# The last output tile of a two-layer MLP kernel in two column pieces, 320 and 128 wide

## Chip, cores and metric

The kernel runs on one core of one Trainium2 chip. It is written instruction by instruction: each engine has its own list of work, and semaphores order the lists against one another. The metric is the device time of one execution in microseconds (us). Four executions of the kernel before gave 93.84, 93.88, 93.94 and 94.49 us; the median is 93.91 us.

The engines are TensorE (PE in the profile; its weight loads are PEld), VectorE (DVE), ScalarE (ACT), GpSimd (POOL) and SyncE (SP, which issues most transfers here).

## What is computed

```python
B, S, D, F = 1, 2048, 448, 1792      # all tensors bf16
def reference(x, w1, b1, w2, b2):
    h = jnp.einsum("bsd,df->bsf", x, w1) + b1
    h = jax.nn.gelu(h, approximate=True)
    return jnp.einsum("bsf,fd->bsd", h, w2) + b2
```

## The kernel before

The 2048 rows of x are worked in four chunks of 512 (`SC`). Layer 1 of a chunk forms h transposed, with 14 blocks of 128 hidden features on the partitions and 512 rows along the free dimension. ScalarE takes each block out of PSUM with the Gelu and the bias b1 into `g`. Layer 2 multiplies: an output tile has 128 rows of x on its partitions and 448 columns; for each of the 14 feature blocks, 128 columns of `g` are the stationary weights and a row block of `w2_sb` streams through.

**Row halves.** TensorE is used as two halves of 64 rows each, which work side by side. Every product over 128 features is made of two matmuls over 64 features. In a part "a" of Layer 2, bank 0 of the tile's PSUM unit gets its products from row half 0 and bank 1 from row half 1; in part "b" it is the other way round. The two matmuls of a step are issued one behind the other and run at the same time, each with a weight load of its own. `mm` (L209) adds a wait where a bank goes from one half to the other. PSUM has four such units of two banks, given out in turn by `next_unit`.

**Layer 2 of the last chunk** sets the end. Its four tiles are p (tiles 0 and 1, a bank for each), q (tile 2) and r (tile 3). In q and r the 448 columns of one tile are split over the two banks, 224 in each. TensorE's order is written out at L438 to L445: p.a, q.a, p.b, then r's bias product, r.a, q.b, r.b. So the drains and stores of p and q run while TensorE is still busy.

**The drain of r.** When r.b ends, VectorE adds b2 to the first 224 columns (L326) while ScalarE copies the other 224 (L329). ScalarE cannot add a row vector in that copy, so b2 is added into this bank ahead of time by a matmul: `bias` (L286) multiplies a matrix of ones with `b2_z`, a tile that is zero but for one row, which is b2. It uses row half 1, and that row is row 64, filled by VectorE at L424 as soon as b2 has been loaded. When both drains are done, SP issues one store for the tile (L275, called at L331) of 128 rows of 896 B, and the program ends when all stores have arrived (L446).

VectorE, ScalarE and SP each work in the order of their lists. SP's list at the end is the two stores of p, the store of q, the store of r.

Of the kernel before, what the change touches and what calls it, by code (L numbers as in the profile page):

```python
# [6 lines left out]
ALU = mybir.AluOpType  # L7
# [66 lines left out]
def bass_standalone__dense_activation_gelu__prompt_kernel(  # L74
# [8 lines left out]
    B, S, D = x.shape  # L83
    F = w1.shape[1]
    P = 128
    H = P // 2
# [3 lines left out]
    x2, out2 = x[0], out[0]  # L90
    NSC, NST, STC, NFT = S // SC, S // P, SC // P, F // P
# [2 lines left out]
    D3 = KT * P  # L94
    DH = D // 2
    NWARM = 7

    with ExitStack() as es:
        sb = lambda name, shape, dt: es.enter_context(nc.sbuf_tensor(name, shape, dt))
# [6 lines left out]
        w2_sb = sb("w2_sb", [P, NFT, D], BF16)  # L106
# [4 lines left out]
        b2_bc = sb("b2_bc", [P, D], BF16)  # L111
        b2_z = sb("b2_z", [P, D], BF16)
        g = sb("g", [P, NFT, S], BF16)
        out_sb = sb("out_sb", [P, NST, D], BF16)
        unit = [es.enter_context(nc.psum_tensor(f"u{i}", [P, 2, SC], FP32)) for i in range(4)]

        pr = Program(nc, es)
        one = nc.const_aps.tensor(1.0, [P, 1], BF16)
        ones_w = one.broadcast_to([P, P])
# [32 lines left out]
        o0v = out2[0:SC, :].rearrange("(p t) d -> p t d", t=STC)  # L152
# [9 lines left out]
        for c in range(1, NSC):  # L162
            for slot in range(KT + 1):
# [5 lines left out]
            out=ident[:, :], in_=ident[:, :], compare_op=ALU.not_equal, fill=1.0,  # L169
# [4 lines left out]
               after=["b1z"])  # L174
# [11 lines left out]
        def dup_x(s0, s1, after, event):  # L186
            pr.op("vector", lambda e: e.tensor_copy(xT[0:H, KT, s0:s1], xT[H:P, KT, s0:s1]),  # L187
                  after=after, event=event)

        def warm(n, cols=SC):  # L190
            for _ in range(n):
                pr.op("tensor", lambda e: e.matmul(unit[0][:, 0, 0:cols], lhsT=ones_w, rhs=ones_m[:, 0:cols],  # L192
                                                   start=True, stop=True))
# [7 lines left out]
        def next_unit():  # L201
            u = order[0]
            order[0] = (u + 1) % 4
            return u

        def free(u):
            return [busy[(u, i)] for i in (0, 1, 2) if (u, i) in busy]

        def mm(u, lo, half, cols, lhsT, rhs, start, stop, after, event=None, skip=False):  # L209

            after = list(after)
            before = side.get((u, lo))
            if start:
                before = None
            if before is not None and before[0] != half:
                after.append(before[1])
            o = pr.op("tensor", lambda e: e.matmul(  # L217
                unit[u][:, lo, cols], lhsT=lhsT, rhs=rhs, start=start, stop=stop, skip_group_check=skip),
                after=after, event=event)
            side[(u, lo)] = (half, o)  # L220

        class Layer1:


            def __init__(self, c, j):
                self.c, self.j, self.u, self.fresh = c, j, next_unit(), True
                self.skip = c == 0
# [43 lines left out]
                        bias=b1_f[:, ft:ft + 1], scale=1.0), after=[("h", c, ft), "b1"], event=("g", c, ft))  # L271
                    busy[(u, lo)] = ("g", c, ft)

        def store(j, after):
            pr.dma("sync", lambda e: e.dma_start(o0v[:, j, :] if j < STC else out2[j * P:(j + 1) * P, :], out_sb[:, j, :]), "out", after=after)  # L275

        class Layer2:


            def __init__(self, c, tiles, last=False):  # L280
                self.c, self.tiles, self.last, self.u = c, tiles, last, next_unit()
                self.split = len(tiles) == 1
                self.n = DH if self.split else D
                self.fresh = [True, True]

            def bias(self):  # L286
                mm(self.u, 1, 1, slice(0, DH), ones_w[H:P, :], b2_z[H:P, DH:D], True, False, free(self.u) + ["b2z"])
                self.fresh[1] = False

            def part(self, name, fts):  # L290
                c, u, n = self.c, self.u, self.n
                for ft in fts:
                    for lo in (0, 1):
                        j = c * STC + self.tiles[0 if self.split else lo]
                        half = lo if name == "a" else 1 - lo
                        rows = slice(half * H, (half + 1) * H)
                        d0 = lo * DH if self.split else 0
                        fin = name == "b" and ft == NFT - 1
                        after = [("g", c, ft), ("w2", ft - ft % 7)] + (free(u) if self.fresh[lo] else [])
                        mm(u, lo, half, slice(0, n), g[rows, ft, j * P:(j + 1) * P], w2_sb[rows, ft, d0:d0 + n],  # L300
                           self.fresh[lo], fin, after, ("y", c, self.tiles[0], lo) if fin else None)
                        self.fresh[lo] = False
                if name == "b" and NFT - 1 in fts:
                    self.drain()

            def drain(self):
                c, u = self.c, self.u
                y = [("y", c, self.tiles[0], lo) for lo in (0, 1)]
                if not self.split:
                    for lo in (0, 1):  # L310
                        j = c * STC + self.tiles[lo]
                        pr.op("vector", lambda e, lo=lo, j=j: e.tensor_tensor(  # L312
                            out=out_sb[:, j, :], in0=unit[u][:, lo, 0:D], in1=b2_bc[:, :], op=ALU.add),
                            after=[y[lo], "b2"], event=("o", j))
                        busy[(u, lo)] = ("o", j)
                        store(j, [("o", j)])
                    return
                j = c * STC + self.tiles[0]
                if not self.last:
                    pr.op("vector", lambda e: e.tensor_tensor(  # L320
                        out=out_sb[:, j, :].rearrange("p (two h) -> p two h", two=2), in0=unit[u][:, :, 0:DH],
                        in1=b2_bc[:, :].rearrange("p (two h) -> p two h", two=2), op=ALU.add),
                        after=y, event=("o", j))
                    store(j, [("o", j)])
                else:
                    pr.op("vector", lambda e: e.tensor_tensor(  # L326
                        out=out_sb[:, j, 0:DH], in0=unit[u][:, 0, 0:DH], in1=b2_bc[:, 0:DH], op=ALU.add),
                        after=[y[0]], event=("o", j, 0))
                    pr.op("scalar", lambda e: e.copy(out_sb[:, j, DH:D], unit[u][:, 1, 0:DH]),  # L329
                          after=[y[1]], event=("o", j, 1))  # L330
                    store(j, [("o", j, 0), ("o", j, 1)])  # L331

# [53 lines left out]

        warm(NWARM)
        warm(1, HC)  # L390
# [5 lines left out]
        for i in (0, 1):  # L396
# [3 lines left out]
                  after=[("w1r", i)], event=("w1rU", i))  # L400
# [13 lines left out]
        for c in range(NSC):  # L414
            if c:
                items = [Layer1(c, j) for j in range(NPAIR)]
                items[0].a()
                for j in range(1, NPAIR):
                    items[j].a()
                    items[j - 1].b()  # L420
                items[-1].b()
            else:

                pr.op("vector", lambda e: e.tensor_copy(b2_z[H:H + 1, :], b2_bc[H:H + 1, :]),  # L424
                      after=["b2", "b2z0"], event="b2z")
            if c + 1 < NSC:
                dup_x((c + 1) * SC, (c + 2) * SC, [("xT", c + 1)], ("xTd", c + 1))
            head, tail, every = range(0, 10), range(10, NFT), range(NFT)
            p = Layer2(c, (0, 1))
            if c + 1 < NSC:  # L430
                q = Layer2(c, (2, 3))
                for part in (head, tail):
                    p.part("a", part)
                    q.part("a", part)
                p.part("b", every)
                q.part("b", every)
            else:
                q, r = Layer2(c, (2,)), Layer2(c, (3,), True)  # L438
                p.part("a", every)
                q.part("a", every)  # L440
                p.part("b", every)
                r.bias()
                r.part("a", every)
                q.part("b", every)
                r.part("b", every)  # L445
        pr.barrier("sync", ["out"])  # L446
        pr.emit()

# [27 lines left out]
```

## Time and profile before

| | |
|---|---|
| median of four executions | 93.91 us |
| profiled execution, its own time | 93.94 us |
| its span in the profile | 92.63 us |
| TensorE matmuls, busy | 89.5 us (97%) |
| granted TensorE clock | 1.0 in all 40 slices |
| first matmul of the last three parts | 86.12 us |
| last VectorE drain starts | 90.44 us |
| store, from issue to landing | 1.7 us (median of 16) |

The span runs from the first to the last recorded event; the profiled execution took 1.3 us more than its span. A busy share is an average, and a matmul's recorded duration includes the way through the array: neighbours overlap, so a rate is read from the distance of two starts. In the rows of a timeline the columns are start, duration (of the whole group from its first start to its last end), engine, line, operation, output and inputs, shapes, and how many. "L63 SPq" are the waits that SP carries out as instructions of their own.

### The profile page before, as it was taken

The page shows a single profiled execution, that of the slowest core. Times are in us where ns is not written, and L with a number is a line of the kernel's source. Part 1 is how long each engine was busy: PE and PEld are TensorE (multiplying, and loading weights), DVE is VectorE, ACT ScalarE, POOL GpSimd, SP SyncE. Part 2 cuts the span into 40 slices and gives each one's busy share as a digit, 9 for nine tenths or more (in the row PEclk, how much of TensorE's full clock was granted, in tenths as well). Part 3 has the DMA queues.
Part 4 walks back from the last instruction along what each step waited for, and adds up shares of the span by engine and source line. Part 5 has one row for each costly group of instructions (what it writes and reads, how often), then busy time and mean ns, then how long its engine had stood idle before and what let it go on. Part 6 is the DMA issues. An engine that isn't in the chain of part 4 may idle for free.

```text
span 92.6 us, 2086 instructions
## 1 busy us (share of the span) xinstructions
PE 89.5 (97%) x945; PEld 46.0 (50%) x945; DVE 13.5 (15%) x34; ACT 38.3 (41%) x64; POOL 1.7 (2%) x8
## 2 busy tenths in 40 slices
PE   6999999999999999999999999999999999999990
PEld 2374444555544444555544444555554444475890
DVE  0166000110441000000433000000333000000421
ACT  6064978600005787700003787900002888900001
POOL 6000000000000000000000000000000000000000
PEclk9999999999999999999999999999999999999999
DMA  2999995964666000000033000000022000000022
GB/s 37 341 268 299 380 348 52 192 120 91 84 107 209 0 7 0 0 0 0 0 102 103 0 4 0 7 0 0 0 99 99 7 0 0 0 0 7 24 75 99
DMA packets 12744, 7.32 MB, mean 79 GB/s; under 512 B 6976, under 2 KB 12544, under 8 KB 12736
## 3 DMA queue, kind: packets, MB, share of 16 engines
q1 hardware_dynamic: 11904, 6.80, 31.1%
q10 hardware_dynamic: 800, 0.39, 1.4%
q8 instruction: 7, 0.11, 0.5%
q0 software_dynamic: 32, 0.00, 0.0%
q14 instruction: 1, 0.01, 0.0%
HBM read 3.79 MB, written 1.84 MB: 61 GB/s over the span
## 4 chain that ended last, share of the span: by engine, by line
PE 97%; DVE 0%; issue 0%
PE u L217 92%; PE u L192 4%; PE u L344 1%; DVE out_sb L326 0%
## 5 line engine op out<-in xcount | busy, mean ns | idle before, releaser
L269 ACT ACTIVATE g<-u,b_f 128x512 bf16<-128x512 f32 x56 | 34.8, 685 | 39.4 <-PE u L217 38.0
L217 PE MATMUL u<-w_sb,g 64*128 64x448 bf16 (+1 forms) x504 | 43.2, 328 | 0.0
L217 PE MATMUL u<-xT,w_sb 64*128 64x512 bf16 (+1 forms) x348 | 41.2, 370 | 0.0
L217 PEld LDWEIGHTS u<-w_sb,g 64*128 64x128 bf16 x504 | 24.5, 94 | 18.4
L217 PEld LDWEIGHTS u<-xT,w_sb 64*128 64x128 bf16 x348 | 16.9, 94 | 19.1 <-DMA w_sb<-in_w_dram 0.4
L312 DVE TENSOR_TENSOR out_sb<-u,b_bc 128x448 bf16<-128x448 f32 x14 | 8.1, 619 | 59.7 <-PE u L217 59.7
L217 PE MATMUL u<-xT,w1r 64*128 64x512 bf16 x56 | 10.6, 376 | 0.0
L217 PEld LDWEIGHTS u<-xT,w1r 64*128 64x128 bf16 x56 | 2.7, 94 | 3.3
L329 ACT CAST out_sb<-u 128x224 bf16<-128x224 f32 x1 | 0.3, 345 | 9.2 <-PE u L217 9.2
L192 PE MATMUL u<-const-bfloat16-1.0 128*128 128x512 bf16 (+1 forms) x8 | 3.4, 598 | 0.8 <-PEq L461 0.8
L192 PEld LDWEIGHTS u<-const-bfloat16-1.0 128*128 128x128 bf16 x8 | 1.0, 136 | 2.4 <-issue 2.4
L357 ACT COPY xT<-u 128x256 bf16<-128x256 bf16 x3 | 1.0, 374 | 2.4 <-PE u L344 2.4
L175 ACT ACT_TABLE_LOAD x1 | 1.3, 1283 | 0.7 <-PEq L461 0.7
L424 DVE COPY b_z<-b_bc 1x448 bf16<-1x448 bf16 x1 | 0.3, 268 | 7.0 <-DMA b_bc<-in_b_dram 7.0
L344 PEld LDWEIGHTS u<-ident,xn 64*128 64x128 bf16 x24 | 0.8, 121 | 0.8 <-issue 0.8
L187 DVE COPY xT<-xT 64x512 bf16<-64x512 bf16 x3 | 0.9, 290 | 2.4 <-DMA xT<-in_x_dram 2.3
L344 PE MATMUL u<-ident,xn 64*128 64x64 bf16 x24 | 1.0, 228 | 0.1
L384 ACT COPY xT<-u 64x256 bf16<-64x256 bf16 x2 | 0.7, 368 | 0.7 <-DVE xT L357 0.6
L357 DVE COPY xT<-u 128x256 bf16<-128x256 bf16 x3 | 0.8, 291 | 1.0 <-PE u L344 1.0
L320 DVE TENSOR_TENSOR out_sb<-u,b_bc 128x448 bf16<-128x448 f32 x1 | 0.6, 623 | 1.7 <-PE u L217 1.7
L181 DVE STREAM_TRANSPOSE b1t<-b1n 32x32 bf16<-32x32 bf16 x4 | 0.8, 202 | 0.1
L362 DVE COPY xr<-xn 128x256 bf16<-128x256 bf16 x1 | 0.2, 227 | 3.2 <-DMA xn<-in_x_dram 3.2
(18 smaller groups left out, 4.7 us busy)
## 6 DMA issues: line engine op xcount, KB each, us to landing
out_dram<-out_sb SPq DMA_DIRECT2D x16, 112.0 KB, 1.7
w_sb<-in_w_dram SPq DMA_DIRECT2D x2, 784.0 KB, 9.2
w_sb<-in_w_dram SPq DMA_DIRECT2D x1, 576.0 KB, 6.2
xn<-in_x_dram SPq DMA_DIRECT2D x1, 448.0 KB, 3.4
w_sb<-in_w_dram ACTq DMA_DIRECT2D x2, 192.0 KB, 4.1
w_sb<-in_w_dram SPq DMA_DIRECT2D x1, 384.0 KB, 5.4
xT<-in_x_dram SPq DMA_TRANSPOSE x12, 4.2
w1r<-in_w_dram SPq DMA_DIRECT2D x1, 160.0 KB, 5.3
```

Of the source, the lines that this page charges most:

```text
L175: pr.op("scalar", lambda e: e.activation(junk[:, :], one, ACT.Gelu_apprx_tanh), event="table")
L181: pr.op("vector", lambda e, q=q: e.transpose(b1t[32 * q:32 * q + 32, :], b1n[:, 32 * q:32 * q + 32]), after=["b1n"], event=("b1t", q))
L187: pr.op("vector", lambda e: e.tensor_copy(xT[0:H, KT, s0:s1], xT[H:P, KT, s0:s1]), after=after, event=event)
L192: pr.op("tensor", lambda e: e.matmul(unit[0][:, 0, 0:cols], lhsT=ones_w, rhs=ones_m[:, 0:cols], start=True, stop=True))
L217: o = pr.op("tensor", lambda e: e.matmul(unit[u][:, lo, cols], lhsT=lhsT, rhs=rhs, start=start, stop=stop, skip_group_check=skip), after=a ...
L269: pr.op("scalar", lambda e, lo=lo, ft=ft: e.activation(g[:, ft, c * SC:(c + 1) * SC], unit[u][:, lo, :], ACT.Gelu_apprx_tanh, bias=b1_f[:, ...
L312: pr.op("vector", lambda e, lo=lo, j=j: e.tensor_tensor(out=out_sb[:, j, :], in0=unit[u][:, lo, 0:D], in1=b2_bc[:, :], op=ALU.add), after= ...
L320: pr.op("vector", lambda e: e.tensor_tensor(out=out_sb[:, j, :].rearrange("p (two h) -> p two h", two=2), in0=unit[u][:, :, 0:DH], in1=b2_ ...
L329: pr.op("scalar", lambda e: e.copy(out_sb[:, j, DH:D], unit[u][:, 1, 0:DH]), after=[y[1]], event=("o", j, 1))
L344: pr.op("tensor", lambda e, half=half, rows=rows: e.transpose(o(half), i(rows), ident[rows, rows]), after=["ident"] + after, event=event i ...
L357: pr.op(engine, lambda e, i=i: (e.copy if engine == "scalar" else e.tensor_copy)(o[:, i], f[:, i]), after=[wait or ("xt", h, ks[-1])], eve ...
L384: e.copy(o, i) if engine == "scalar" else e.tensor_copy(o, i),
```

## The change

The last tile is worked as two pieces. r now has columns 0 to 319, 160 in each of its two banks; a new piece t has columns 320 to 447, 64 in each bank, in a PSUM unit of its own. Each piece has its drains on VectorE and ScalarE and its own store. TensorE's order becomes p.b, the bias products of r and of t, r.a, q.b, t.a, r.b, t.b. r's bias product runs on row half 1 as before, over 160 columns; t's on row half 0, over 64. For the latter, row 0 of `b2_z` is filled with b2 too, by one more small copy on VectorE. `store` takes a column range; `cols` gives the column range of a bank; `done` names the event of a finished bank.

```diff
+    LAST = 160
...
-        def store(j, after):
-            pr.dma("sync", lambda e: e.dma_start(o0v[:, j, :] if j < STC else out2[j * P:(j + 1) * P, :], out_sb[:, j, :]), "out", after=after)
+        def store(j, after, d0=0, d1=D):
+            rows = o0v[:, j, d0:d1] if j < STC else out2[j * P:(j + 1) * P, d0:d1]
+            pr.dma("sync", lambda e: e.dma_start(rows, out_sb[:, j, d0:d1]), "out", after=after)
...
-            def __init__(self, c, tiles, last=False):
-                self.c, self.tiles, self.last, self.u = c, tiles, last, next_unit()
+            def __init__(self, c, tiles, d0=0, n=D):
+                self.c, self.tiles, self.d0, self.n, self.u = c, tiles, d0, n, next_unit()
                 self.split = len(tiles) == 1
-                self.n = DH if self.split else D
+                self.last = self.split and n < DH
                 self.fresh = [True, True]
 
-            def bias(self):
-                mm(self.u, 1, 1, slice(0, DH), ones_w[H:P, :], b2_z[H:P, DH:D], True, False, free(self.u) + ["b2z"])
+            def cols(self, lo):
+                d = self.d0 + lo * self.n if self.split else 0
+                return slice(d, d + self.n)
+
+            def bias(self, half):
+                rows = slice(half * H, (half + 1) * H)
+                mm(self.u, 1, half, slice(0, self.n), ones_w[rows, :], b2_z[rows, self.cols(1)], True, False,
+                   free(self.u) + ["b2z"])
                 self.fresh[1] = False
...
-                        mm(u, lo, half, slice(0, n), g[rows, ft, j * P:(j + 1) * P], w2_sb[rows, ft, d0:d0 + n],
-                           self.fresh[lo], fin, after, ("y", c, self.tiles[0], lo) if fin else None)
+                        mm(u, lo, half, slice(0, n), g[rows, ft, j * P:(j + 1) * P], w2_sb[rows, ft, self.cols(lo)],
+                           self.fresh[lo], fin, after, self.done(lo) if fin else None)
...
                     pr.op("vector", lambda e: e.tensor_tensor(
-                        out=out_sb[:, j, 0:DH], in0=unit[u][:, 0, 0:DH], in1=b2_bc[:, 0:DH], op=ALU.add),
-                        after=[y[0]], event=("o", j, 0))
-                    pr.op("scalar", lambda e: e.copy(out_sb[:, j, DH:D], unit[u][:, 1, 0:DH]),
-                          after=[y[1]], event=("o", j, 1))
-                    store(j, [("o", j, 0), ("o", j, 1)])
+                        out=out_sb[:, j, d0:d1], in0=unit[u][:, 0, 0:n], in1=b2_bc[:, d0:d1], op=ALU.add),
+                        after=[self.done(0)], event=("o", j, d0))
+                    pr.op("scalar", lambda e: e.copy(out_sb[:, j, d1:d2], unit[u][:, 1, 0:n]),
+                          after=[self.done(1)], event=("o", j, d1))
+                    store(j, [("o", j, d0), ("o", j, d1)], d0, d2)
...
-                pr.op("vector", lambda e: e.tensor_copy(b2_z[H:H + 1, :], b2_bc[H:H + 1, :]),
-                      after=["b2", "b2z0"], event="b2z")
+                for row in (0, H):
+                    pr.op("vector", lambda e, row=row: e.tensor_copy(b2_z[row:row + 1, :], b2_bc[row:row + 1, :]),
+                          after=["b2", "b2z0"], event="b2z" if row else None)
...
-                q, r = Layer2(c, (2,)), Layer2(c, (3,), True)
+                q = Layer2(c, (2,), 0, DH)
+                r, t = Layer2(c, (3,), 0, LAST), Layer2(c, (3,), 2 * LAST, DH - LAST)
                 p.part("a", every)
                 q.part("a", every)
                 p.part("b", every)
-                r.bias()
+                r.bias(1)
+                t.bias(0)
                 r.part("a", every)
                 q.part("b", every)
+                t.part("a", every)
                 r.part("b", every)
+                t.part("b", every)
```

Here `n` is the columns per bank, and `d0`, `d1 = d0 + n`, `d2 = d0 + 2 * n` are a piece's column bounds.

More of the change, by code (lines that the diff above doesn't have):

```diff
@@ L296, in part @@
                         rows = slice(half * H, (half + 1) * H)
-                        d0 = lo * DH if self.split else 0
                         fin = name == "b" and ft == NFT - 1
                         after = [("g", c, ft), ("w2", ft - ft % 7)] + (free(u) if self.fresh[lo] else [])
-                        mm(u, lo, half, slice(0, n), g[rows, ft, j * P:(j + 1) * P], w2_sb[rows, ft, d0:d0 + n],
-                           self.fresh[lo], fin, after, ("y", c, self.tiles[0], lo) if fin else None)
+                        mm(u, lo, half, slice(0, n), g[rows, ft, j * P:(j + 1) * P], w2_sb[rows, ft, self.cols(lo)],
+                           self.fresh[lo], fin, after, self.done(lo) if fin else None)
                         self.fresh[lo] = False
@@ L304, in part, with done @@
                     self.drain()
+            def done(self, lo):
+                return ("y", self.c, self.tiles[0], self.d0, lo)
             def drain(self):
-                c, u = self.c, self.u
-                y = [("y", c, self.tiles[0], lo) for lo in (0, 1)]
+                u, n = self.u, self.n
                 if not self.split:
                     for lo in (0, 1):
-                        j = c * STC + self.tiles[lo]
+                        j = self.c * STC + self.tiles[lo]
                         pr.op("vector", lambda e, lo=lo, j=j: e.tensor_tensor(
                             out=out_sb[:, j, :], in0=unit[u][:, lo, 0:D], in1=b2_bc[:, :], op=ALU.add),
-                            after=[y[lo], "b2"], event=("o", j))
+                            after=[self.done(lo), "b2"], event=("o", j))
                         busy[(u, lo)] = ("o", j)
@@ L317, in drain @@
                     return
-                j = c * STC + self.tiles[0]
+                j = self.c * STC + self.tiles[0]
+                d0, d1, d2 = self.d0, self.d0 + n, self.d0 + 2 * n
                 if not self.last:
                     pr.op("vector", lambda e: e.tensor_tensor(
[L321 to L324, printed above, removed]
+                        out=out_sb[:, j, d0:d2].rearrange("p (two h) -> p two h", two=2), in0=unit[u][:, :, 0:n],
+                        in1=b2_bc[:, d0:d2].rearrange("p (two h) -> p two h", two=2), op=ALU.add),
+                        after=[self.done(0), self.done(1)], event=("o", j, d0))
+                    store(j, [("o", j, d0)], d0, d2)
                 else:
                     pr.op("vector", lambda e: e.tensor_tensor(
-                        out=out_sb[:, j, 0:DH], in0=unit[u][:, 0, 0:DH], in1=b2_bc[:, 0:DH], op=ALU.add),
-                        after=[y[0]], event=("o", j, 0))
-                    pr.op("scalar", lambda e: e.copy(out_sb[:, j, DH:D], unit[u][:, 1, 0:DH]),
-                          after=[y[1]], event=("o", j, 1))
-                    store(j, [("o", j, 0), ("o", j, 1)])
+                        out=out_sb[:, j, d0:d1], in0=unit[u][:, 0, 0:n], in1=b2_bc[:, d0:d1], op=ALU.add),
[3 more added lines that the diff above has]
+                    store(j, [("o", j, d0), ("o", j, d1)], d0, d2)
         HALVES = (slice(0, H), slice(H, P))
```

## The prediction

> **What bounds the kernel now.** I read the totals and the chain of the page first, then the matmuls of the last 7 us, then the timeline after the last one.
>
> ```profile
> span 92.6 us, 2086 instructions
> PE 89.5 (97%) x945; PEld 46.0 (50%) x945; DVE 13.5 (15%) x34; ACT 38.3 (41%) x64; POOL 1.7 (2%) x8
> ...
> PE 97%; DVE 0%; issue 0%
> PE u L217 92%; PE u L192 4%; PE u L344 1%; DVE out_sb L326 0%
> ```
>
> TensorE is the bound from start to end; only a last addition on VectorE (L326) hangs behind it, and behind that the last store. So the change can act in two places: TensorE's time in the last three parts, and the tail from the last matmul to the span's end. The timeline of the last microseconds, and the store's own waits and transfer:
>
> ```profile
> 90.44 0.39 DVE L326 TENSOR_TENSOR out_sb<-u,b_bc 128x224 bf16<-128x224 f32 x1 [0.61 <-PE u L217]
> 90.48 0.34 ACT L329 CAST out_sb<-u 128x224 bf16<-128x224 f32 x1 [9.23 <-PE u L217]
> ...
> SPq L63 <- DMA out_dram<-out_sb: 1.4, 1, 1.4
> SPq L63 <- ACT out_sb L329: 0.6, 1, 0.6
> ...
> 91.15:91.70 0.55, 0.00 (x0) 0.00 (x0) 0.00 (x0) 0.00 (x0) 0.00 (x0) 1.00 0.00 0
> 91.70:92.25 0.55, 0.00 (x0) 0.00 (x0) 0.00 (x0) 0.00 (x0) 0.00 (x0) 1.00 0.65 209
> 92.25:92.63 0.38, 0.00 (x0) 0.00 (x0) 0.00 (x0) 0.00 (x0) 0.00 (x0) 1.00 0.00 0
> ```
>
> (The last three rows are stretches; their last two columns are DMA share and GB/s.) With the single stamps of the trace, the tail is: last matmul starts 90.150, VectorE 90.443 to 90.833, ScalarE 90.477 to 90.822, SP issues the store at 90.912, packets run from 91.742 to about 92.24, the last completion arrives at 92.595, the span ends at 92.628. In the transfer only the half microsecond with packets depends on size: 16 engines with 8 packets of 896 B each, 39 to 49 ns apart. The 0.83 us before and 0.37 us after it are latency.
>
> **TensorE, worked out.** A part is 14 steps of two matmuls, one on each row half, running side by side. In the trace the 224-column pairs start 95.8 ns apart. Two other pairs can be seen at this clock: 448 columns at 189 ns, 512 at about 216 ns. All are (columns / 2.4) + 2.4 ns. For r's 160 columns I take 66.7 + 2.4 = 69.1 ns. For t's 64 columns the nearest row is the transposes through the identity at the start: the same 64x128 weight load for each, and 64 moving columns:
>
> ```profile
> 5.55 0.23 PE L344 MATMUL u<-ident,xn 64*128 64x64 bf16 x4
> ...
> 5.60 0.23 PE L344 MATMUL u<-ident,xr 64*128 64x64 bf16 x4
> ```
>
> Four start in 58 ns, 14.6 ns each, so 29.1 ns a pair, again 64 / 2.4 + 2.4. (The twenty before them, from 4.25 us on, start 26.6 ns apart: there every matmul still streams at half this rate.) It is a short row, eight in line, and they transpose where t accumulates; hence the rivals.
>
> Row half 1 carries the old bias product alone, and so it ends one slot later: 84 of the 85 matmuls stand in pairs, the last starts alone at 90.150. Half 1 of before, from 86.122: bias, r.a, q.b, r.b = 43 x 95.8 = 4.119 us. After: bias of r 69.1 ns; r.a and r.b 28 x 69.1 = 1.935 us; q.b 14 x 95.8 = 1.341; t.a and t.b 28 x 29.1 = 0.815; sum 4.160 us. Half 0, which gets t's bias, is 40 ns shorter. So 28 more pairs cost only 28 times 2.4 ns, less 27 ns from the narrower bias product: **+41 ns**. The last matmul itself is shorter: 190 ns for a 64-column record, 256 for 224 columns. Its end is at 90.253 + 0.190 = 90.443, against 90.406: **+37 ns**.
>
> Here a rule of the Trainium skill speaks against the change. Its page "TensorE: Matmul & The Clock Gate", section "Back-to-back issue gap", says that starts never come closer than about 25 ns however few the columns, and that a sustained stream of weight load and matmul at 128 columns runs at about 81 ns per matmul. By the first, taken per matmul, a pair of t costs 50 ns, 28 pairs 1.40 us instead of 0.815. By the second, taken per pair, 28 x 81 = 2.27 us. The row (14.6 ns between starts with two halves in use, 3 ns within the 224-column pairs) contradicts the first as a limit per matmul; per row half, 29.1 ns lies above it. I take the row; both figures go into the range.
>
> **The drains.** VectorE's 448 columns take 619 ns and 224 take 390, 1.02 ns a column; so 160 columns 325 ns and 64 columns 227 ns. ScalarE's 224 take 345; with 0.84 to 1.18 ns a column (against the 128x256 copy of 374 and the 128x512 Gelu of 685) 64 columns are 155 to 210 ns, 160 some 280. t: VectorE starts 37 ns later than before, 90.480, and ends 90.707; ScalarE 90.514 to about 90.70. So t's data are ready **126 ns earlier** than the 90.833 of before.
>
> **The stores, and SP between them.** r.b ends 407 ns (14 x 29.1) ahead of t.b. Its last matmul starts at 86.122 + 3.752 - 0.069 = 89.805 and ends 229 ns later, 372 ns before the old end. Its drains therefore run 90.071 to 90.396 on VectorE, with t's addition queued behind and 84 ns to spare. SP issued 79 ns after the drains before, so r's store goes out at 90.475. An issue holds SP:
>
> ```profile
> L275 SPq DMA_DIRECT2D out_dram<-out_sb x16: 332/333/582, 27.1 to 90.9; - x16
> ```
>
> 332 ns, to 90.807; then 45 ns to the next instruction (as between the loads at the start: 44 to 50 ns), and t's store has a separate wait instruction ahead of it, 64 ns. t's store goes out at **90.916**. Its data would have allowed 90.786. So r's own issue uses up what the smaller drain gains, and the issue stays where it was, 90.912. That is the step at which the gain is lost, and it would be worth 130 ns without it.
>
> What is left is the transfer. t's rows are 256 B. No store of this size is in the trace; packets of 256 B into the chip (the transposing loads and b1) take 18 ns, of 512 B 27 ns, of 896 B 41. 8 x (45 - 18) = **216 ns less** before the completions. The two ends: nothing, if a short write takes as long as a long one, and 0.2 us to the bad if short writes are slower still. For the latter speaks the skill's page "DMA: Bandwidth & Descriptors", section "Specifications": a transfer below 512 B is done as read-modify-write, where line rate needs 512 B. It gives no time, and no run here shows a short write; the rows that the kernel stores now start at multiples of 128 B, so they too have ragged ends without visible harm. I take the 18 ns. r's packets (about 32 ns) run from 91.305 to some 91.66, before t's first at 91.746, so the two don't compete.
>
> **Edits at nothing.** The second one-row copy to b2_z costs 268 ns of VectorE at 16.46 us; the next work there (the copy of x at L187) comes at 18.78, waiting for its load. Without that cover it would cost its 268 ns there, not at the end. q.b ends some 0.37 us earlier; its addition and store move along and leave SP free before 90.475. The accumulator of t was last read by the Gelus that end at 81.24, five microseconds before t's bias. Half-to-half waits of r and t find their products 28 matmuls old. 116 more TensorE instructions are some 5% of its stream, whose code is loaded in seven pieces beside the work today without a gap at the end.
>
> **Sum**, in the profiled execution: 90.916 + (92.628 - 90.912) - 0.216 = 92.416, **0.21 us** less than its span of 92.63. Its own time is 93.94, 1.31 us around the span; I carry the difference over to the median of 93.91: **93.70 us**, 0.2% faster. This is less than the 0.5% (0.47 us) which I take as what a measurement of this kernel can tell from no change.
>
> **Rivals.**
> - *The short packets win nothing* (writes are bound by something else than bytes). For it: no such write is in the trace. Against: packet time follows bytes in four sizes. Then the time is 93.91 + 0.00, at worst +0.2 with read-modify-write: 93.9 to 94.1.
> - *t's short matmuls are slower in a long run* (the other side): weight loads, issue or accumulation set a floor of c ns a pair in place of 29. r's store is late by 14(c - 29), t's data by 28(c - 29) with 130 ns in hand. The change loses from 28(c - 29) - 130 = 216, c = 41 ns, on, and 0.47 us from c = 58 ns. At 50 ns (25 per matmul): 458 - 216 = +0.24, 94.15. At 81 ns: 1326 - 216 = +1.11, 95.0. For it: 56 in line, where the trace shows 8; 256 and 448 columns never test it. Against: those eight needed two instructions per 14.6 ns with the same loads, and TensorE has the instructions of t waiting while it is bound by streams.
> - *SP is not the limit* (r's issue overlaps with t's wait): another 0.13 us, 93.57. The trace never shows two stores closer than 465 ns, so I hold it small.
> - *The tail doesn't respond at all*, time as before: inside the first rival.
>
> **Chances.** My forecast 0.58, first rival 0.16 (a fifth of it, with read-modify-write worse than I bound it, beyond 94.38), short matmuls slow 0.16 (two thirds of it beyond 94.38), SP free 0.05, and 0.05 for a latency of the transfer that shrinks with its size as well and takes the time below 93.44. So faster by over 0.5% 0.05, slower by over 0.5% 0.03 + 0.11 = 0.14, within 0.5% the remaining 0.81. The range starts at SP free less 0.07 for the spread of the closest three executions, 93.50, and goes up to 94.15, where read-modify-write and the floor of 25 ns lie; what stays out is the floor of 81 ns, the worst short writes and the shrinking latency, some 0.18.
>
> **What the profile after would show.** Right: 64-column matmuls in pairs 29 ns apart, 160-column ones 69; VectorE's last addition near 227 ns starting near 90.48; two stores on SP 0.44 us apart, the second at about 90.92; 256 B packets of some 18 ns; a span near 92.42. Wrong: gaps in the 64-column stretch; a last addition that waits longer; a second store later than 90.95; or packets of 256 B at 40 ns and more, or a completion later than 0.37 us after them.

## The result

The changed kernel takes 94.35 us (median of 35 executions), the kernel before 93.93 us (median of 56 in the same comparison): **0.38% slower**, ratio 1.0038 with a 95% interval of 1.0023 to 1.0053. Forecast were 93.70 us and 0.2% faster, with a range that ended at 94.15. The size of the change is within the 0.5% of the forecast's likeliest class; the sign is wrong, and the time lies outside the range.

First the page of the changed kernel, the line of its span and three of its transfer queues (packets, MB, share of the 16 engines; q1 carries SP's stores, q10 ScalarE's transfers):

```profile
span 93.0 us, 2205 instructions
...
q1 hardware_dynamic: 12048, 6.80, 29.1%
q10 hardware_dynamic: 800, 0.39, 1.4%
q8 instruction: 8, 0.13, 0.6%
```

The kernel before has in the last place:

```profile
q8 instruction: 7, 0.11, 0.5%
```

q8 loads instruction code, in packets of 16 KB. There is one more of them, and this turns out to be the answer. The groups of the changed kernel's last 7 us, shapes kept apart (busy time in us, mean ns of one):

```profile
L218 PE MATMUL u<-w_sb,g 64*128 64x160 bf16 x56 | 2.3, 229 | 0.0
...
L218 PE MATMUL u<-w_sb,g 64*128 64x64 bf16 x56 | 1.2, 190 | 0.0
...
L336 DVE TENSOR_TENSOR out_sb<-u,b_bc 128x160 bf16<-128x160 f32 x1 | 0.3, 324 | 0.6 <-PE u L218 0.6
...
L336 DVE TENSOR_TENSOR out_sb<-u,b_bc 128x64 bf16<-128x64 f32 x1 | 0.2, 224 | 0.1
L339 ACT CAST out_sb<-u 128x64 bf16<-128x64 f32 x1 | 0.2, 212 | 0.1
```

All of these durations are as forecast, to a few nanoseconds. The two last stores in the timeline are not (start, duration of the issue on SP):

```profile
90.45 0.94 SPq L277 DMA_DIRECT2D out_dram<-out_sb  x1
...
91.49 0.38 SPq L277 DMA_DIRECT2D out_dram<-out_sb  x1
```

r's store is issued at 90.45 us, where the forecast had 90.475, but the issue takes 940 ns and not 332. t's data are ready at 90.69 us; SP comes to t's store at 91.49. The same stretch in windows (last columns: TensorE clock, DMA share, GB/s):

```profile
90.65:91.15 0.50, 0.00 (x0) 0.00 (x0) 0.02 (x1) 0.04 (x1) 0.00 (x0) 1.00 0.04 7
91.15:91.70 0.55, 0.00 (x0) 0.00 (x0) 0.00 (x0) 0.00 (x0) 0.00 (x0) 1.00 0.06 10
91.70:92.25 0.55, 0.00 (x0) 0.00 (x0) 0.00 (x0) 0.00 (x0) 0.00 (x0) 1.00 0.49 147
92.25:92.63 0.38, 0.00 (x0) 0.00 (x0) 0.00 (x0) 0.00 (x0) 0.00 (x0) 1.00 0.40 90
```

A DMA share of 0.06 is one transfer engine of 16. The queue of the code loads has one packet in the stretch from 89.95 to 91.03 us, and its 6.2% of 16 engines' time is one engine for the whole stretch:

```profile
q8 instruction: 1, 0.02, 6.2%
```

The single packets' stamps in the trace give the order: the new code load runs from 89.958 to 91.024 us, and eight of the 128 packets of q's store, one engine's share, start only from 91.010 on, while the other 120 have started by 90.68. SP is released at 91.393, when that engine is at the fourth of them.

Executions differ in how long they wait for the first loads. To compare them I use a **tail** from here on: the time from the start of p's first addition on VectorE to the end of the span, in the one profiled execution of each kernel. It is 6.306 us in the kernel before and 6.743 in the changed one, 437 ns more, like the medians.

### The profile page after: what moved, and what is told of

Read it like the earlier page. It is cut to its first block, busy times and chain, and to the rows that moved or that the text cites. A ratio compares the mean times of both kernels' runs of the same rounds, so it can differ in the third digit from the quotient of the medians.

```text
span 93.0 us, 2205 instructions
## 1 busy us (share of the span) xinstructions
PE 89.2 (96%) x1002; PEld 46.0 (49%) x1002; DVE 13.9 (15%) x36; ACT 38.5 (41%) x65; POOL 1.7 (2%) x8
## 4 chain that ended last, share of the span: by engine, by line
PE 92%; DMA 4%; issue 0%; DVE 0%; ACT 0%
PE u L218 92%; DMA xn<-in_x_dram 4%; PE u L354 0%; DVE xT L367 0%; ACT out_sb L339 0%
## 5 line engine op out<-in xcount | busy, mean ns | idle before, releaser
L218 PE MATMUL u<-w_sb,g 64*128 64x448 bf16 (+3 forms) x560 | 43.2, 312 | 0.0
L339 ACT CAST out_sb<-u 128x160 bf16<-128x160 f32 (+1 forms) x2 | 0.5, 252 | 9.0 <-PE u L218 8.9
```

The costliest lines, as they stand in the source:

```text
L218: o = pr.op("tensor", lambda e: e.matmul(unit[u][:, lo, cols], lhsT=lhsT, rhs=rhs, start=start, stop=stop, skip_group_check=skip), after=a ...
L339: pr.op("scalar", lambda e: e.copy(out_sb[:, j, d1:d2], unit[u][:, 1, 0:n]), after=[self.done(1)], event=("o", j, d1))
```

## The experiments

Theory A: the late code load holds up SP's issue of r's store. Theory B: rows of 640 B at a pitch of 896 B are slow to issue. The first runs tell them apart. Ratios are to the kernel before, measured in the same comparison, with the 95% interval in brackets.

**after_shift: the load elsewhere.** The code loads come at nearly fixed places of TensorE's list (by count, below). More instructions at its start bring the last one earlier in the work.

```diff
-        warm(NWARM)
-        warm(1, HC)
+        warm(80, 48)
```

> The changed kernel, with the warm-up of TensorE at the start cut into 80 matmuls of 48 columns in place of 7 of 512 and one of 256: the same columns, 144 more instructions, so that the eighth load of TensorE's code is asked for 144 instructions earlier, near 88.2 us in place of 89.96. Theory A (SP's issue of r's store was held up by that code load): the issue takes about 332 ns in place of 940, t's store goes out near 90.9, the span is about 92.4 and the time about 93.7. Theory B (rows of 640 B at a pitch of 896 B are slow to issue): the issue still takes about 940 ns, the time stays at 94.35.

93.80 us, ratio 0.9973 (0.9955 to 0.9990). The load runs from 88.14 to 89.32 us. The issues on SP:

```profile
91.04 0.33 SPq L277 DMA_DIRECT2D out_dram<-out_sb  x1
...
91.47 0.38 SPq L277 DMA_DIRECT2D out_dram<-out_sb  x1
```

r's issue is at 333 ns, with the same 640 B rows. The tail is 6.145 us, 161 ns shorter than before. The sign of the forecast is back.

> The changed kernel with the 80 short warm-up matmuls once more, beside the others, as the measure for the ScalarE store and to see its gain over the kernel before a second time. Theory A: 0.2% to 0.3% faster than before, 93.7 to 93.8. Theory B: 94.35.

The repeat gave 93.86 us, ratio 0.9981 (0.9957 to 1.0005), and again a tail of 6.145 us.

**before_shift: its control**, the same edit in the kernel before.

> The control: the kernel before with the same 80 short warm-up matmuls. It now has an eighth code load too, near 87.8 us, between the stores of p and that of q. Both theories: the last store is issued as before in about 332 ns, and the time is that of the kernel before, 93.9, unless the warm-up itself costs something, which this run would show.

Ratio 0.9998 (0.9977 to 1.0018), tail 6.308 us, an eighth load at 88.53 us. The short warm-up matmuls give and cost nothing; neither does a code load that meets no issue.

**before_two_stores: the split store alone.**

```diff
-                    store(j, [("o", j, 0), ("o", j, 1)])
+                    store(j, [("o", j, 0), ("o", j, 1)], 0, 320)
+                    store(j, [("o", j, 0), ("o", j, 1)], 320, D)
```

(`store` takes a column range here as in the change.)

> The kernel before, with its last tile stored in two transfers of 320 and 128 columns, one behind the other; TensorE and the drains are untouched and there is no eighth code load. Theory A: the issue of the 640 B rows takes about 332 ns, the second follows at about 91.29, its packets of 256 B save 0.2 us, and the span is about 92.8, the time about 94.1. Theory B: the first issue takes about 940 ns, the second starts near 91.9, and the time is about 94.7.

```profile
91.41 0.33 SPq L276 DMA_DIRECT2D out_dram<-out_sb  x1
...
91.78 0.43 SPq L276 DMA_DIRECT2D out_dram<-out_sb  x1
```

332 ns for the 640 B rows: theory B falls. 94.24 us, ratio 1.0023 (1.0000 to 1.0045), tail 6.561 us, 255 ns longer: 375 for the second store's later issue and 103 for its own longer one, less 220 for its shorter rows. A second store right behind the first costs its issue; r's store in the change goes out ahead of the last data and costs far less of it (105 ns, under after_shift_act).

**before_load and before_load2: the late load in the kernel before.** The warm-up was cut into 32 matmuls of 120 and 36 of 107 columns.

> The kernel before with the warm-up as 32 matmuls of 120 columns, 48 more instructions, which should put an eighth code load near 90.05 us, over the issue of the last store at 90.91. Nothing else differs. Theory A: that issue ends some 0.35 us after the code load does, near 91.5 in place of 91.24, and the time rises by 0.1 to 0.3 us to 94.0 to 94.2. Theory B: the issue takes 332 ns as before and the time stays at 93.9.

> The kernel before with the warm-up as 36 matmuls of 107 columns: 56 more instructions. The control with 144 more had its eighth code load 2.28 us before TensorE's end, which is 95 instructions, so that some 49 are needed for one to come at all; 56 should bring it about 0.17 us before the end, and with its 0.9 to 1.4 us it covers the issue of the last store, which comes 0.76 us after the last matmul starts. Theory A: that issue takes 0.5 to 0.9 us in place of 0.33, and the time rises by 0.2 to 0.6 us over the kernel before, to 94.1 to 94.5. Theory B: 0.33 us and no change in time.

Both missed: no eighth load came, and the times are those of the kernel before (0.9993, interval 0.9976 to 1.0009; and 0.9996, 0.9981 to 1.0011). I had counted in time from the end; the count that holds is in matmuls. The seventh load starts at matmul 838 to 848 in these two kernels, the kernel before and the changed one, the eighth, in the kernels that have one, at 970 to 974, or at 985 and 986 where it falls among t's short matmuls (before_p_load, below, is the exception at 958). These two kernels have 969 and 973 matmuls in all.

**after_act: t's store on ScalarE's queue, load in place.**

```diff
-            pr.dma("sync", lambda e: e.dma_start(rows, out_sb[:, j, d0:d1]), "out", after=after)
+            pr.dma("scalar" if d0 == 2 * LAST else "sync",
+                   lambda e: e.dma_start(rows, out_sb[:, j, d0:d1]), "out", after=after)
```

> The changed kernel as it is, with the late code load, but with t's store issued by ScalarE. If a code load holds up only SP's transfers, t's store is issued in 0.33 us from about 90.75 and lands near 92.3, and the end is r's store, near 92.65: about 94.0. If it holds up ScalarE's transfers as well, t's issue ends no earlier than about 91.4 and the span is 92.7 to 92.9, the time 94.1 to 94.25.

```profile
90.25 0.85 SPq L278 DMA_DIRECT2D out_dram<-out_sb  x1
...
90.57 0.36 ACTq L278 DMA_DIRECT2D out_dram<-out_sb  x1
```

The load runs from 89.77 to 90.84 us. SP is held again, 854 ns, and released 0.26 us behind the load; ScalarE is not: its issue takes 362 ns, against 366 in the next run, where no load is near. The tail is 6.336 us, and its end is r's store. 94.18 us, ratio 1.0012 (0.9991 to 1.0033). The trace shows the first of the two cases that I had written down; the time lies in the range of the second.

**after_shift_act: both edits.**

> The changed kernel with the 80 short warm-up matmuls and with t's store issued by ScalarE, behind its own copy, in place of SP. If SP's issue of r's store is what holds t's store back (0.13 us by the prediction), t's store goes out about 0.12 us after its data and the time falls by some 0.1 us against the same kernel with the store on SP, to about 93.7. If both queues share what issues them, r's issue (333 ns from about 91.04) still stands before it and the time is the same 93.8.

```profile
90.73 0.33 SPq L278 DMA_DIRECT2D out_dram<-out_sb  x1
...
91.06 0.37 ACTq L278 DMA_DIRECT2D out_dram<-out_sb  x1
```

93.70 us, ratio **0.9966** (0.9949 to 0.9982), the fastest of all. The tail is 6.040 us, 105 ns less than with t's store on SP. So r's own issue is what holds t's store once the load is out of the way, at about the price that the forecast gave (130 ns). The two intervals overlap; the step between these two kernels rests on the traces.

**after_full, before_full, after_full_act: fewer instructions.** Layer 2 of the second chunk in matmuls over all 128 rows, one for each pair.

```diff
-                for ft in fts:
+                full = c == 1
+                for ft in fts if not (full and name == "b") else ():
...
-                        half = lo if name == "a" else 1 - lo
-                        rows = slice(half * H, (half + 1) * H)
+                        half = 2 if full else lo if name == "a" else 1 - lo
+                        rows = slice(0, P) if full else slice(half * H, (half + 1) * H)
```

(Part "b" is empty then, and `fin` is set in part "a".)

> The changed kernel, with Layer 2 of the second chunk done in matmuls over all 128 rows, one in place of each pair of two row halves: 112 matmuls for 224, so 112 instructions fewer in TensorE's list than the changed kernel has, 946 matmuls in all as in the kernel before, and no eighth code load at the end. The arithmetic is the same. Theory A: r's store is issued in 332 ns and the end is that of the prediction, 93.7 us, provided a full-row matmul of 448 columns takes the 189 ns of a pair. Theory B: 94.35.

> The control: the kernel before with the same full-row matmuls in the second chunk. It shows what these cost or gain by themselves. Expected 93.9, as the kernel before, and seven code loads or fewer; if a weight load of 128 rows is not hidden behind the matmul before it, up to 50 ns more for each of 112, that is up to 5 us.

> The changed kernel with the full-row matmuls in the second chunk and with t's store issued by ScalarE. If both work as in the runs before, the store goes out some 0.1 us earlier than on SP and the time is about 93.6.

before_full is slower by itself: 1.0034 (1.0015 to 1.0052). Its full-row matmuls of 448 columns run at the rate of a pair, but two starts are late where the work changes between halves and full rows, 308 and 285 ns apart in place of some 190; that is 0.2 us of the 0.32. The rest I did not trace. after_full is at 0.9996 (0.9973 to 1.0019), after_full_act at 0.9994 (0.9970 to 1.0017): against the kernel before they win nothing, and the 93.7 and 93.6 us that I expected were missed. Against their control both gain 0.4%, as theory A has it, and in after_full_act, which has no eighth load, r's issue takes 333 ns and the tail is 6.039 us, that of after_shift_act. For after_full only the time is used.

**What holds SP.** ScalarE's queue was not held beside the load, SP's was. The remaining question was whether SP is held by any code load, or only where a store of its own still waits on the engine that the load occupies.

> The kernel before with the warm-up as 116 matmuls of 33 columns, 108 more than before. The code loads start at a fixed place in TensorE's list (matmul 838 and 972 or so in the runs above, whatever is ahead of them), so the eighth now starts some 80 matmuls before the end, near 86.4 us, over the issue of p's first store near 87.0; rows of 896 B, no split tile. Theory A: one of p's two issues takes 0.5 to 1.1 us in place of 0.33, and the time is not touched by it, since q's store comes 2 us later. Theory B: all issues take 332 ns. The warm-up may itself take longer, since it has a weight load for every 33 columns.

This one missed: with 116 warm-up matmuls of 33 columns the load came at matmul 958 and was over at 85.95 us, and p's first issue came at 86.77. 94.03 us, ratio 1.0004 (0.9981 to 1.0026).

> The kernel before with 98 warm-up matmuls of 39 columns, 90 more than before, which should bring the eighth code load near 86.6 us, over the issue of p's two stores (86.97 and 87.50). SP has no store in flight when p's first is issued. If a waiting share in SP's own queue is what holds SP, the first issue takes 332 ns and the second, or neither, is long; if any issue during a code load is held, the first is long, 0.5 to 1.1 us. The time is the one of the kernel before in both cases.

```profile
87.29 0.33 SPq L275 DMA_DIRECT2D out_dram<-out_sb  x1
...
87.82 1.20 SPq L275 DMA_DIRECT2D out_dram<-out_sb  x1
```

The load runs from 87.36 to 88.64 us. p's first issue is at its 332 ns, with 0.26 us of the load in it; the second, with the first store still waiting, takes 1198 ns and ends 0.38 us behind the load. These are whole rows of 896 B in the kernel before. The time is not touched, ratio 0.9992 (0.9966 to 1.0019), as expected: q's store is 2 us away.

**after_q_act: SP's queue empty.** q's store is issued by ScalarE, everything else as in the changed kernel.

```diff
-            pr.dma("sync", lambda e: e.dma_start(rows, out_sb[:, j, d0:d1]), "out", after=after)
+            pr.dma("scalar" if j == NST - 2 else "sync",
+                   lambda e: e.dma_start(rows, out_sb[:, j, d0:d1]), "out", after=after)
```

> The changed kernel with its late code load in place, warm-up as it was, but with q's store issued by ScalarE, which has been idle for 8 us, in place of SP. In the trace of the changed kernel the code load occupies one of the 16 transfer engines from 89.96 to 91.02, and that engine's eight packets of q's store start only behind it, at 91.01. If SP is held because q's share is still waiting in SP's own queue on that engine, SP's queue is empty here and r's issue takes 332 ns; then only the packets that lie on that engine are late, and the time is 93.7 to 94.0. If any issue by SP during a code load is held, it takes 0.85 to 0.95 us again and the time stays near 94.3.

```profile
90.57 0.33 SPq L278 DMA_DIRECT2D out_dram<-out_sb  x1
...
91.00 0.40 SPq L278 DMA_DIRECT2D out_dram<-out_sb  x1
```

The load runs from 90.08 to 91.08 us, straight over r's issue, and that takes 332 ns. So it is not the load alone: SP was held in the three places above where a store of its own had packets behind the load, and not here, where the late packets were in ScalarE's queue.

Four more held issues are in these traces, all at the first stores of the output, near 27 to 28 us, in the kernels with 80 short warm-up matmuls, whose third code load falls there. In after_shift (minimum, median and maximum of the issue in ns):

```profile
L277 SPq DMA_DIRECT2D out_dram<-out_sb x17: 332/332/1345, 26.7 to 91.5; - x17
```

The others took 1141 (after_shift_again), 1234 (after_shift_act) and 1399 ns (before_shift), each with transfers of SP's own in flight. No cost in time shows: before_shift is at 0.9998. Two issues were not held although SP's own packets were on their way: both began just before a load ended. In before_load2 it was 0.12 us before, at 69.757 us, with eight packets of SP's earlier store behind that load, and the issue took 332 ns; in after_q_act it is t's issue at 91.00, 0.07 us before, with 400 ns. The seven held issues outlasted the load by 0.26 to 0.38 us, so a wait for these packets alone does not explain both kinds, and the exact condition stays open.

The tail of after_q_act is 6.244 us, 62 ns less than before. The median of 94.30 us, ratio 1.0021 (0.9998 to 1.0043), does not show that gain. The code loads of these traces take from 0.88 to 1.7 us, and the shares of q, r and t on the occupied engine all wait for it; whether that explains the difference was not tested.

## Why the prediction was wrong

By its own steps, on the common scale of the tail, in after_shift where the load is away:

- **TensorE: right.** 64-column pairs start 29 ns apart over a whole part of 14 pairs (in the changed kernel's last part the single matmuls start 14 and 15 ns apart), and 160-column pairs 69.2 ns apart. The last matmul starts 109 ns later than before against p's drain; forecast were 103 (90.253 less 90.150). The floor of 25 ns per matmul and the 81 ns of a weight-loaded stream (the Trainium skill, "TensorE: Matmul & The Clock Gate", "Back-to-back issue gap") do not bind two row halves: single starts are closer than the first, and 160-column pairs closer than the second. Within one row half, 29 ns stays above the first. The row of eight transposes was the better guide.
- **Drains: right.** 324 and 224 ns on VectorE (325, 227), 292 and 212 on ScalarE (280, 155 to 210).
- **SP between the stores: right in size.** 431 ns from r's issue to t's, forecast 441. after_shift_act shows that the rest of the slack is there.
- **The short rows: nearly right.** 17 ns a packet (18), and from the end of its issue the store of 256 B rows lands in 1.15 us where that of 896 B rows took 1.37: 220 ns, forecast 216. But t's issue itself takes 378 ns, 46 more than 332. No price of read-modify-write (the skill's page "DMA: Bandwidth & Descriptors", "Specifications") shows: packets of 256 B into the chip took 18 ns too.
- Sum: t's store goes out 13 ns later than r's did before (forecast 4), its issue takes 46 ns more, and it lands 220 ns sooner behind that: 161 ns less, forecast 212.
- **The step that failed stands under "Edits at nothing"**: that 116 more instructions are some 5% of a stream "whose code is loaded in seven pieces beside the work today without a gap at the end". I looked for a gap on TensorE, and there is none. The count was not made (nor is 116 quite right: 57 matmuls with a weight load each are 114). Seven loads in 945 matmuls, the last at matmul 838 and the others 118 to 128 apart after the second, so an eighth was due near 966, and the changed kernel has 1002. The eighth starts in the last half microsecond of TensorE's work, at matmul 985, with q's store on its way and r's about to be issued. The term is 940 - 332 = **608 ns** on SP; with it the sum is -161 + 608 = +447, and the tail measured is +437. The prediction's own sign of being wrong, a second store later than 90.95, came true at 91.49, by a cause that it does not name.

How far this is shown: that the late load turns the gain into a loss rests on the times of after_shift and its control before_shift. That it does so through SP's issue rests on one trace of each kernel. Since after_q_act has no held issue and its median is still not below before's, a part of the loss may come by another way, such as the late packets themselves; that stays open.

The trace of before has signs of the effect, in the transposing loads of x that SP issues (minimum, median and maximum of the issue in ns):

```profile
L147 SPq DMA_TRANSPOSE xT<-in_x_dram x12: 1261/1262/2167, 9.3 to 25.8; - x12
```

The one of 2167 ns starts at 13.87 us, while a code load runs from 13.67 to 14.77; another, of 1858 ns, starts at 22.60 with a load from 22.23 to 23.41. They are not proof by themselves: two others, of 1652 and 1480 ns at 9.34 and 11.04, have no code load beside them. The prediction does not speak of these issues. The rival with the sharpest loss, slow short matmuls, has the right sign and the wrong mechanism.

## What to carry to other kernels

When a change adds instructions to an engine's list, count where its code loads fall, before and after, and lay them beside the transfers issued there: near the end of a kernel a new load can cost more than the work that was added, while the same held issue in the middle of these kernels cost nothing. A load that falls badly can be moved by instructions elsewhere in the list that cost no time, as in after_shift. And a transfer's issue with a maximum far above its median is a row to explain, not to average.

## What the runs showed of the hardware

- A code load of 16 KB takes 0.9 to 1.7 us here on one of 16 transfer engines, and one comes about every 128 matmuls with their weight loads (88 to 128 apart in the kernel before). The Trainium skill's page "Runtime: NRT & Kernel Launch", section "Instruction fetch mechanics", gives the 16 KiB and the 256 instructions, and calls the cost of crossing such a boundary mostly hidden. The size agrees; the cost was 0.6 us on another engine's queue in the changed kernel.
- Packets of any store that lie on that engine wait for the load: eight of 128 in the changed kernel, after_act and after_q_act. SP was held as well in seven of the nine store issues that it began during a load with transfers of its own still in flight: 854 to 1399 ns, where the last stores take 332 without a load, ending 0.26 to 0.38 us behind the load. It was not held when its queue was empty (332 ns, after_q_act), nor was ScalarE beside SP's late packets (362 ns, after_act), nor SP in the two issues begun in the last 0.12 us of a load (332 ns in before_load2, 400 in after_q_act). That its own packets behind the load are the reason is inferred from these cases; the inside of the queue isn't in the trace.
- Matmuls of 64 moving columns with a weight load each ran on two row halves at one start per 14.6 ns in the changed kernel's last part, 28 in line. As a pair of halves, that is 29 ns.
